# Loads of keys and values on GpSimd's queue, attention one step later, and four unsplit steps

## The chip, the cores and the metric

The kernel runs on one core of one Trainium2 chip. The metric is the device time of one execution in microseconds. The core's engines are TensorE (PE in the profile; its weight loads are PEld), VectorE (DVE), ScalarE (ACT), GpSimd (POOL) and SyncE (SP). SyncE does no arithmetic here; it issues DMAs. GpSimd and ScalarE can issue DMAs too, each through a queue of its own.

## The reference

Three stages follow one another, all in float32.

- Attention with pooled keys and values: q, k and v have the shape (8 batches, 8 heads, 576 positions, 64). Keys and values are averaged over groups of 8 positions, which leaves 72 of each. Then softmax(q k^T / 8) v per batch and head.
- A first layer on the 4608 tokens x 512 features: `h = x @ w_in` (512 x 2048), then g = h for h >= 1, 0 for h <= -1, and (h + 1)^2 / 4 in between, then `g @ w_out` (2048 x 512).
- A second layer of the same sizes with g = max(h, 0)^2.

## The kernel before

**Split products.** A float32 product on TensorE would be slow, so each operand is split into a high part that TensorE takes in its faster format and a low part, the rest. A product is then three matmuls: high x high, low x high, high x low. The high part is made by ScalarE (a copy) and the low part by VectorE (a subtraction). In the trace these are `wihi` and `wilo` for the first weight of a layer, `wohi` and `wolo` for the second (both L237 and L241), `xhi` and `xlo` for the tokens (L541, L542) and `gh` and `gl` for the activations (L749, L755). `WHOLE` (L26) says how many of the very first steps leave the second product unsplit: those multiply `gw` and `wo` in plain float32 (L775), and make none of `gh`, `gl`, `wohi`, `wolo`.

**Steps.** The first layer is done in steps: 9 blocks of 512 tokens x 16 slices of 128 hidden features, 144 steps, and then the first block of the second layer in 16 more. In step s TensorE does the first product of step s (`gemm1`, L714, 12 matmuls) and the second product of step s - 2 (`gemm2`, L786, 12 matmuls, or L775). The result of a block stands in four PSUM banks (`acc`) until its last step. The rest of the second layer (from about 1000 us) has another form and isn't touched.

**Weights of the first layer.** They come in pieces of 512 KB through SyncE's queue (`st`, `stx`, L135 and L140), and ScalarE and VectorE convert them to their final values (`convert_w`, L147) in the first 16 steps, some 8 pieces ahead of the step that uses them. The second layer's weights are converted later, from step 28 on; there an integer addition runs on GpSimd (L182), ScalarE copies its result (`cb`, L192) and it is stored for later.

**Attention beside the steps.** The 4608 tokens are 36 tiles of 128. Tiles 0 to 3 are done ahead of step 0, in an order written out by hand (`before`). The tiles from the fourth on are put into the steps: each step has two slots, 2s after its first product and 2s + 1 after its second. A tile t has units for the scores of heads 0 to 3 and 4 to 7 (`s`), for the next tile's queries (`q`), and for its output (`x`). For tiles 4 to 7 the slots are listed; from tile 8 on they follow from one number `c` (L562): scores at 2c and 2c + 2, queries at 2c + 4, output at 2c + 11. The output of a block's four tiles is the input of that block's first product, so the last of them has to be out before step 16j for block j. Where a tile is the first with a new batch, its keys' units stand at 2c - 2 and 2c - 1, and the pooling of that batch's keys and values (`pool_kv`, VectorE, L332 and L333) at slots counted from c (`pool_at`).

**Keys and values.** `load_kv` loads a pair of heads into one of three buffers `kv` (a fourth place is borrowed for the last pair of batch 0). For batches 0 and 1 the pooling is done by TensorE with a matrix of ones (`pk` L346 for keys, `pv` L367 for values), and each pair is two transfers, a large one (L303, 256 KB) and one of the last 64 positions (L313, 32 KB; batch 0 has one for all heads). For batches 2 to 7 a pair is one transfer (L317, 288 KB) and VectorE pools. A load waits until its buffer has been read for the last time.

**What sets the order.** The program order is that of the Python code, but a planner rearranges it: it keeps a priority by program order, assumes a duration for each instruction, and puts on each engine and each queue what it believes ready first. That order is then fixed, and on the chip every engine and every queue works strictly in it. So an instruction that waits holds all that stands behind it in its queue, and a unit may run some steps ahead of its slot.

Of the kernel before, what the change touches and what calls it, by code (L numbers as in the profile page):

```python
# [22 lines left out]
LEAD = 8  # L23
HEADS = 3

WHOLE = 6  # L26

TURNED = 8

# [5 lines left out]
def pooled_attention_moe_moe(  # L35
# [11 lines left out]
    nc = tc.nc  # L47
# [8 lines left out]
    KF = DFF // P  # L56
# [235 lines left out]
    def load_kv(nm, b, p):  # L292
        if b == 0 and p == NP - 1:

            a = cv.tile([P, 2, POOL * D], F32, tag="st", name="kv")
        else:
            a = kvp.tile([P if b < ON_PE else SP, 2, POOL * D], F32, tag="kv", name="kv")
        src = k if nm == "k" else v
        kv_t[nm, b, p] = a
        if b < ON_PE:  # L300

            src = src[b, 2 * p:2 * p + 2]
            nc.sync.dma_start(  # L303
                out=a[:, :, 0:BY * D], in_=src[:, 0:BY * P, :].rearrange("h (s r) d -> s h (r d)", r=BY)
            )
            if b == 0:
                if p == (1 if nm == "k" else 0):
                    rest[nm] = gp.tile([S - BY * P, H, D], F32, tag="gh", name="rest")
                    nc.sync.dma_start(
                        out=rest[nm], in_=(k if nm == "k" else v)[b, :, BY * P:S, :].rearrange("h s d -> s h d")  # L310
                    )
                return
            nc.sync.dma_start(  # L313
                out=a[0:S - BY * P, :, BY * D:(BY + 1) * D], in_=src[:, BY * P:S, :].rearrange("h s d -> s h d")
            )
            return
        nc.sync.dma_start(  # L317
            out=a, in_=src[b, 2 * p:2 * p + 2].rearrange("h (s r) d -> s h (r d)", r=POOL)
        )

# [228 lines left out]
    TB0 = TB // P  # L549
# [6 lines left out]
    for t in range(TB0, NTILE):  # L556

        if t < 2 * TB0:
            c = (2, 5, 8, 10)[t - TB0]
            at_s0, at_s1, at_q, at_x = 2 * c, 2 * c + 1, 2 * c + 2, (15, 19, 25, 29)[t - TB0]  # L560
        else:
            c = KF - 4 + 4 * (t - 2 * TB0)  # L562
            at_s0, at_s1, at_q, at_x = 2 * c, 2 * c + 2, 2 * c + 4, 2 * c + 11
        todo = {at_s0: ("s", t, 0), at_s1: ("s", t, 1), at_x: ("x", t)}
        if t == 2 * TB0 - 1:
            todo[at_x - 2] = ("all", ("p", t, 0), ("p", t, 1))
        if t + 1 < NTILE:
            todo[at_q] = ("q", t + 1)
        if t in first_tile:
            b = first_tile.index(t)  # L570
            todo.update({2 * c - 2 + i // 2: ("k", b, i) for i in (0, 2)})
            if b < ON_PE:
                todo.update({at_v: ("v", b, i) for at_v, i in zip((7, 9), (0, 2))})
            for i in range(2 * NP if b >= ON_PE else 0):
                at_p = 2 * (c + i - 8) + (i >= NP) * 8
                pool_at[at_p] = 2 * NP * b + i + 1
        assert not slots.keys() & todo.keys()
        slots.update(todo)

        assert 2 * KF * (t // TB0 - 2) <= at_x - 2 < at_x + 2 < 2 * KF * (t // TB0), t  # L580
# [9 lines left out]
    def load_kv_to(n):  # L590
        while kv_loaded[0] < min(n, len(kv_order)):
            load_kv(*kv_order[kv_loaded[0]])
            kv_loaded[0] += 1
# [78 lines left out]
    def whole(kind, s):  # L672

        return kind == "o" and s < WHOLE

# [411 lines left out]
    def temp(tag, bufs=2):  # L1087
        return tp.tile([P, TB], F32, tag=tag, name=tag, bufs=bufs)
# [109 lines left out]
    for n, u in enumerate(units):  # L1198
        kind, b, i, g = u
# [9 lines left out]
        if kind == "i":  # L1209
            if i == 5:  # L1210
                after_i(b, 5, g)

                c = temp("c", 3)
# [42 lines left out]
```

## Time and profile before

| | |
|---|---|
| time, median of 3 runs | 1620.85 us (1620.62 to 1620.98) |
| profiled execution | 1620.48 us, its span 1618.7 us |
| TensorE busy | 1612.0 us (100%), 7866 matmuls |
| weight loads of TensorE | 1317.1 us (81%) |
| VectorE busy | 1246.5 us (77%) |
| ScalarE busy | 905.0 us (56%) |
| GpSimd busy | 54.1 us (3%), 60 instructions |
| DMA moved | 283.91 MB, 175 GB/s on the mean |
| SyncE's queue (q1) | 249072 packets, 282.16 MB |
| granted TensorE clock | full in all slices of the span |

The span is the time from the first to the last instruction; the few microseconds around it belong to the execution too. Matmuls overlap in the records: one of 512 columns is recorded with about 390 ns, but follows the one before it after some 227 ns, so a busy share of TensorE near 100% means that it never stood, and the length of a group is read from the starts. An unsplit float32 matmul is recorded as two. GpSimd issues no DMA in this kernel: all loads and stores but four at the end go through SyncE's queue.

### The profile page before, as it was taken

The page shows a single profiled execution, that of the slowest core. Times are in us where ns is not written, and L with a number is a line of the kernel's source. Part 1 is how long each engine was busy: PE and PEld are TensorE (multiplying, and loading weights), DVE is VectorE, ACT ScalarE, POOL GpSimd, SP SyncE. Part 2 cuts the span into 40 slices and gives each one's busy share as a digit, 9 for nine tenths or more (in the row PEclk, how much of TensorE's full clock was granted, in tenths as well). Part 3 has the DMA queues.
Part 4 walks back from the last instruction along what each step waited for, and adds up shares of the span by engine and source line. Part 5 has one row for each costly group of instructions (what it writes and reads, how often), then busy time and mean ns, then how long its engine had stood idle before and what let it go on. Part 6 is the DMA issues. An engine that isn't in the chain of part 4 may idle for free.

```text
span 1618.7 us, 23331 instructions
## 1 busy us (share of the span) xinstructions
PE 1612.0 (100%) x7866; PEld 1317.1 (81%) x7866; DVE 1246.5 (77%) x2231; ACT 905.0 (56%) x1676; POOL 54.1 (3%) x60
## 2 busy tenths in 40 slices
PE   9999999999999999999999999999999999999998
PEld 7678888888878888888888888888888888888887
DVE  6999889898898999998975542578558855975585
ACT  7786566666666666666775532345335533553353
POOL 0000000100000000010100000000000000000000
PEclk9999999999999999999999999999999999999999
DMA  9753344554454554543560474566776776758565
GB/s 257 233 176 99 96 127 151 167 163 120 133 157 147 170 146 132 170 136 134 183 220 7 133 264 148 193 218 207 200 251 220 217 229 210 222 184 252 194 206 142
DMA packets 250279, 283.91 MB, mean 175 GB/s; under 512 B 123440, under 2 KB 155824, under 8 KB 250160
## 3 DMA queue, kind: packets, MB, share of 16 engines
q1 hardware_dynamic: 249072, 282.16, 56.5%
q8 instruction: 63, 1.03, 0.3%
q14 instruction: 56, 0.46, 0.1%
q10 hardware_dynamic: 1088, 0.26, 0.1%
HBM read 217.71 MB, written 64.62 MB: 174 GB/s over the span
## 4 chain that ended last, share of the span: by engine, by line
PE 98%; DMA 1%; DVE 1%; SPq 0%; issue 0%; ACT 0%; DVEq 0%; ACTq 0%
PE ph L714 27%; PE acc L786 26%; PE cp L1072 11%; PE dp L1081 10%; PE dq L1081 5%; PE cr L1072 5%; PE dr L1081 3%; PE cq L1072 3%; PE pss L411 2%; PE px L529 2%; PE acc L775 1%; PE pv L367 0%; DMA kv<-in_v_dram 0%; DMA w<-w2i 0%; PE pk L346 0%; PE dp L1182 0%
## 5 line engine op out<-in xcount | busy, mean ns | idle before, releaser
L714 PE MATMUL ph<-xhi,wihi 128*128 128x512 f32 x576 | 229.9, 399 | 0.0
L1029 ACT ACTIVATE gh<-g 128x512 fp32r<-128x512 f32 x224 | 139.9, 630 | 152.9 <-DVE g L1098 47.9
L714 PE MATMUL ph<-xlo,wihi 128*128 128x512 f32 x576 | 225.0, 391 | 0.0
L714 PE MATMUL ph<-xhi,wilo 128*128 128x512 f32 x576 | 224.9, 390 | 0.0
L786 PE MATMUL acc<-gh,wohi 128*128 128x512 f32 x552 | 222.6, 403 | 0.0
L786 PE MATMUL acc<-gl,wohi 128*128 128x512 f32 x552 | 216.1, 391 | 0.0
L786 PE MATMUL acc<-gh,wolo 128*128 128x512 f32 x552 | 215.5, 390 | 0.0
L821 DVE TENSOR_TENSOR gl<-g,gh 128x512 fp32r<-128x512 f32 x224 | 151.9, 689 | 49.7 <-ACT gh L1029 48.2
L1072 PE MATMUL cp<-x,w 128*128 128x512 f32 x768 | 186.4, 390 | 0.2 <-DMA w<-w2i 0.2
L1072 PEld LDWEIGHTS cp<-x,w 128*128 128x128 f32 x768 | 143.9, 188 | 31.5 <-ACT s L1094 1.4
L237 ACT ACTIVATE wihi<-wi 128x512 fp32r<-128x512 f32 x144 | 90.6, 629 | 123.4 <-PE ph L714 122.7
L1081 PE MATMUL dp<-gh,w 128*128 128x512 f32 x496 | 156.8, 390 | 0.0
L241 DVE TENSOR_TENSOR wilo<-wi,wihi 128x512 fp32r<-128x512 f32 x144 | 101.9, 708 | 46.5 <-ACT wihi L237 43.5
L714 PEld LDWEIGHTS ph<-xhi,wihi 128*128 128x128 f32 x576 | 108.1, 188 | 26.7 <-issue 3.8
L714 PEld LDWEIGHTS ph<-xhi,wilo 128*128 128x128 f32 x576 | 108.2, 188 | 23.1 <-issue 0.2
L714 PEld LDWEIGHTS ph<-xlo,wihi 128*128 128x128 f32 x576 | 108.3, 188 | 21.1 <-issue 0.2
L755 DVE TENSOR_TENSOR gl<-g,gh 128x512 fp32r<-128x512 f32 x154 | 107.0, 695 | 23.1 <-ACT gh L749 20.4
L749 ACT ACTIVATE gh<-g 128x512 fp32r<-128x512 f32 x138 | 86.8, 629 | 64.4 <-DVE g L747 63.5
L1094 ACT ACTIVATE s<-cp 128x512 f32<-128x512 f32 x96 | 57.1, 595 | 116.8 <-PE cp L1072 116.0
L786 PEld LDWEIGHTS acc<-gl,wohi 128*128 128x128 f32 x552 | 103.7, 188 | 22.9
L786 PEld LDWEIGHTS acc<-gh,wohi 128*128 128x128 f32 x552 | 103.8, 188 | 20.9 <-issue 0.6
L786 PEld LDWEIGHTS acc<-gh,wolo 128*128 128x128 f32 x552 | 103.9, 188 | 19.9
(161 smaller groups left out, 2953.3 us busy)
## 6 DMA issues: line engine op xcount, KB each, us to landing
w<-w2i SPq DMA_DIRECT2D x224, 256.0 KB
w<-w2o SPq DMA_DIRECT2D x224, 256.0 KB
w2i<-cb SPq DMA_DIRECT2D x32, 512.0 KB
w2o<-cb SPq DMA_DIRECT2D x32, 512.0 KB
st<-in_moe_w_in_dram SPq DMA_DIRECT2D x30, 512.0 KB
st<-in_moe_w_out_dram SPq DMA_DIRECT2D x30, 512.0 KB
pd<-pad SPq DMA_DIRECT2D x31, 384.0 KB
z<-pd SPq DMA_DIRECT2D x93, 128.0 KB
```

What stands on the lines that cost most here:

```text
L237: nc.scalar.activation(out=hi, in_=src, func=AF.Copy)
L241: eng.tensor_tensor(out=lo, in0=src, in1=hi.bitcast(F32), op=ALU.subtract)
L411: nc.tensor.matmul(out=pss[off:off + n, i, :], lhsT=qT[t][:, p, off:off + n], rhs=kbd[b % 2][:, p, :], start=True, stop=True,)
L714: nc.tensor.matmul(out=ph, lhsT=a[:, kk % a.shape[1], :], rhs=c[:, kk, :], start=(i == 0), stop=(i == 3 * KD - 1))
L749: act(out=gh, in_=g, func=AF.Copy)
L755: nc.vector.tensor_tensor(out=gl, in0=g, in1=gh.bitcast(F32), op=ALU.subtract)
L786: nc.tensor.matmul(out=o, lhsT=lhsT, rhs=rhs, start=(f == 0 and x == 0), stop=(f == KF - 1 and x == 2),)
L821: tt(out=out, in0=a, in1=b, op=ALU.subtract)
L1029: act(out=hi, in_=a, func=AF.Copy)
L1072: nc.tensor.matmul(out=out[0], lhsT=w[:, a, k, :], rhs=xq[b, i][c][:, k, :], start=(n == 0 and i in (1, 2, 7)), stop=(n == 5), skip_group_ ...
L1081: nc.tensor.matmul(out=out[d], lhsT=w[:, a, d, :], rhs=x[c], start=(g == 0 and n == 0 and i in (1, 2, 7, 4)), stop=(g == NG - 1 and n == 2 ...
L1094: act(out=snaps[key], in_=a, func=AF.Copy)
```

## The change

Three edits:

1. `WHOLE` goes from 6 to 4, so steps 4 and 5 do their second product split.
2. In `load_kv` the queue is SyncE's for batch 0 and GpSimd's for batches 1 to 7. All six calls of `load_kv`'s transfers use it; buffers, sizes and order stay.
3. `c` of the tiles from the eighth on is one larger, so all their units, the keys' units and the pooling of batches 2 to 7 stand one step (two slots) later. The step at which the attention's buffers are given back moves along, since it is worked out from the last slot.

```diff
-WHOLE = 6
+WHOLE = 4
...
         src = k if nm == "k" else v
+        queue = nc.sync if b == 0 else nc.gpsimd
         kv_t[nm, b, p] = a
         if b < ON_PE:
 
             src = src[b, 2 * p:2 * p + 2]
-            nc.sync.dma_start(
+            queue.dma_start(
                 out=a[:, :, 0:BY * D], in_=src[:, 0:BY * P, :].rearrange("h (s r) d -> s h (r d)", r=BY)
             )
             if b == 0:
                 if p == (1 if nm == "k" else 0):
                     rest[nm] = gp.tile([S - BY * P, H, D], F32, tag="gh", name="rest")
-                    nc.sync.dma_start(
+                    queue.dma_start(
                         out=rest[nm], in_=(k if nm == "k" else v)[b, :, BY * P:S, :].rearrange("h s d -> s h d")
                     )
                 return
-            nc.sync.dma_start(
+            queue.dma_start(
                 out=a[0:S - BY * P, :, BY * D:(BY + 1) * D], in_=src[:, BY * P:S, :].rearrange("h s d -> s h d")
             )
             return
-        nc.sync.dma_start(
+        queue.dma_start(
             out=a, in_=src[b, 2 * p:2 * p + 2].rearrange("h (s r) d -> s h (r d)", r=POOL)
         )
...
         else:
-            c = KF - 4 + 4 * (t - 2 * TB0)
+            c = KF - 3 + 4 * (t - 2 * TB0)
             at_s0, at_s1, at_q, at_x = 2 * c, 2 * c + 2, 2 * c + 4, 2 * c + 11
```

## Rows read from the trace of the kernel before

**Rows 1.** Busy us (instructions) of each engine in three stretches, clock, DMA.
```profile
0.00:40.00 40.00, 38.15 (x334) 31.60 (x335) 26.27 (x62) 28.39 (x80) 2.03 (x10) 1.00 0.95 260
40.00:160.00 120.00, 119.90 (x664) 88.99 (x664) 114.59 (x220) 91.63 (x217) 0.52 (x2) 1.00 0.58 168
160.00:820.00 660.00, 660.00 (x3352) 539.37 (x3351) 588.05 (x1136) 428.90 (x781) 50.41 (x46) 1.00 0.48 147
...
```
**Rows 2.** Chain of waits in order of time, 60 to 100 us: start, us, what.
```profile
63.65 6.36 DMA kv<-in_v_dram
...
82.09 3.44 PE acc L775 x8
88.27 3.43 PE acc L775 x8
...
96.23 2.77 PE acc L786 x12
```
**Rows 3.** Groups of instructions on ScalarE and VectorE: busy us, mean ns, idle before.
```profile
L749 ACT ACTIVATE gh<-g 128x512 fp32r<-128x512 f32 x138 | 86.8, 629 | 64.4 <-DVE g L747 63.5
L237 ACT ACTIVATE wohi<-wo 128x512 fp32r<-128x512 f32 x138 | 85.8, 622 | 13.0 <-PE acc L786 11.1 <-DVE wo L182 1.5
...
L755 DVE TENSOR_TENSOR gl<-g,gh 128x512 fp32r<-128x512 f32 x154 | 107.0, 695 | 23.1 <-ACT gh L749 20.4
L241 DVE TENSOR_TENSOR wolo<-wo,wohi 128x512 fp32r<-128x512 f32 x138 | 96.6, 700 | 5.9 <-ACT wohi L237 5.6
```
**Rows 4.** VectorE in order of time, 71 to 143 us: start us, us, instruction.
```profile
71.31 0.68 DVE L332 TENSOR_TENSOR kv<-kv 72x512 f32<-72x512 f32 x1
...
141.36 0.74 DVE L469 TENSOR_REDUCE sm<-pn 128x8 f32<-128x576 f32 x1
142.01 0.68 DVE L542 TENSOR_TENSOR xlo<-px,xhi 128x512 fp32r<-128x512 f32 x1
```
**Rows 5.** TensorE in order of time around step 16.
```profile
145.11 0.48 PE L714 MATMUL ph<-xhi,wihi 128*128 128x512 f32 x1
```
**Rows 6.** VectorE in order of time, 330 to 338 us.
```profile
330.79 0.67 DVE L542 TENSOR_TENSOR xlo<-px,xhi 128x512 fp32r<-128x512 f32 x1
...
337.24 0.69 DVE L755 TENSOR_TENSOR gl<-g,gh 128x512 fp32r<-128x512 f32 x1
```
**Rows 7.** TensorE in order of time, 339 to 343 us.
```profile
339.18 0.39 PE L714 MATMUL ph<-xhi,wihi 128*128 128x512 f32 x1
...
342.29 0.49 PE L786 MATMUL acc<-gh,wohi 128*128 128x512 f32 x1
```
**Rows 8.** SyncE's queue in order of time, 42 to 64 us.
```profile
42.32 0.38 SPq L303 DMA_DIRECT2D kv<-in_k_dram  x1
...
63.65 0.38 SPq L303 DMA_DIRECT2D kv<-in_v_dram  x1
```
**Rows 9.** Waits of SyncE's queue: us in total, times, longest us.
```profile
SPq L303 <- PE pk L346: 12.1, 2, 11.0
```
**Rows 10.** TensorE in order of time, pooling of batch 1.
```profile
46.61 0.90 PE L346 MATMUL pk<-pad,kv 128*64 128x64 f32 x20
...
59.53 2.79 PE L367 MATMUL pv<-kv,pad 128*72 128x128 f32 x20
...
68.56 2.96 PE L367 MATMUL pv<-kv,pad 128*72 128x128 f32 x20
```
**Rows 11.** Instructions on the tile kv: ns min/median/max, first and last start, forms.
```profile
L332 DVE TENSOR_TENSOR kv<-kv x96: 373/636/1808, 71.3 to 685.7; 72x512 f32<-72x512 f32 x48, 72x256 f32<-72x256 f32 x48
...
L317 SPq DMA_DIRECT2D kv<-in_k_dram x24: 307/400/752, 64.8 to 610.0; - x24
```
**Rows 12.** Instructions of line 182 on GpSimd: ns min/median/max, first and last start.
```profile
L182 POOL TENSOR_TENSOR z<-st,z x16: 1306/1542/2832, 214.8 to 798.2; 128x512 int32<-128x512 int32 x16
```
**Rows 13.** Waits between engines: us in total, times, longest us.
```profile
ACT cb L192 <- POOL z L182: 38.6, 30, 3.2
```

## The prediction

> **What bounds the kernel now.** I read the busy time by stretch first. TensorE is busy for 119.90 of the 120 us from 40 to 160 us, and for 660.00 of 660 us after that, at a granted clock of 1.00 [rows 1]; it loses 1.85 us before 40 us, while the first tiles are prepared. The chain of waits read in order of time says the same: it is a file of matmul groups, with one DMA in it between 60 and 100 us, a load of values that takes 6.36 us [rows 2]. So only two things can pay: fewer TensorE cycles, or the few waits that TensorE still has. And only one thing can cost: work that reaches TensorE too late. VectorE is the engine to watch: 114.59 us of 120 between 40 and 160 us, when the first layer's weights are converted, and 588.05 of 660 us after that [rows 1].
>
> All sums are made against the profiled execution's own 1620.48 us (its span of 1618.70 us and 1.78 us around it). The median of the runs is 1620.85 us, 0.37 us more, and the final number is put on that.
>
> **Part 1: four unsplit steps instead of six.** The second product of an unsplit step is a group of 8 records on TensorE of 3.43 or 3.44 us; the first split one is 12 records of 2.77 us [rows 2]. Steps 4 and 5 (the groups at 82.09 and 88.27 us) change from one to the other: 2 x (3.43 - 2.77) = 1.32 us less. Each of the two steps pays for it elsewhere: two more activations (0.629 us for `gh`, 0.622 us for `wohi`) and two more VectorE operations (0.695 us for `gl`, 0.700 us for `wolo`) [rows 3]. That is 2.50 us for ScalarE, which has 28.37 us idle from 40 to 160 us, and 2.79 us for VectorE, which has 5.41 us [rows 1]. What must be late for TensorE to notice? The tightest hand-over that I found there is the last tile of the second token block (t = 7): its `xlo` starts at 142.01 us and takes 0.68 us, and the first product of step 16, which reads it, starts at 145.11 us, so 2.42 us are left [rows 4, 5]. TensorE gets there 1.32 us earlier, which leaves 1.10 us. If nothing absorbed the 2.79 us of VectorE, TensorE would stand for 2.79 - 1.10 = 1.69 us at step 16. Two things absorb it: the idle 5.41 us, and work of tile 8 that part 2 moves behind this point, such as the sum of its softmax rows (0.74 us at 141.36 us) [rows 4]. The bounds of the stall are 0 and 1.69 us; I take 0, since what is idle is twice what is added. So part 1 is -1.32 us, and +0.37 us at worst.
>
> **Part 2: tiles from the eighth one step later.** No instruction is added or removed. Scores, turned queries, outputs and pooling of each tile get slots that lie one step further on. A step lasts 6.06 us in this stage (step 16's first product starts at 145.11 us, step 48's at 339.18 us: 194.07 / 32) [rows 5, 7]. The hand-over that gets tighter is again that of a block's last tile: tile 15's `xlo` ends at 330.79 + 0.67 = 331.46 us and is read from 339.18 us on, 7.72 us later [rows 6, 7]; one step less leaves 1.66 us. Tile 7, which this part does not move, already sits at just that distance (slot 29, two steps ahead of step 16), in the stretch in which VectorE is fullest, and still has its 2.42 us. So I price part 2 at nothing; the bounds are 0 and, if VectorE ran one 1.8 us operation late at each of the seven later blocks [rows 11], 7 x (1.8 - 1.66) = 1.0 us. Its help for part 1 is not certain either: the planner issues what is ready, and a pooling of batch 2 ran at 71.31 us, in step 5, though its slot is in step 8 [rows 4].
>
> **Part 3: 64 loads of keys and values move from SyncE's queue to GpSimd's.** These are 16 of batch 1 (8 large, 8 small) and 48 of batches 2 to 7. On SyncE the queue stood for 12.1 us in total, 11.0 us in one piece, in front of a load whose buffer TensorE still read [rows 9]; weight loads behind it will now pass. They had landed in time anyway, since TensorE did not wait, so this frees nothing that the path sees. What is on the path are the two loads that come just in time. The first is the last pair of values of batch 1: it was issued at 63.65 us, its buffer is free from about the middle of the pooling at 59.53 us (59.53 + 2.79 / 2 = 60.9 us), and the pooling at 68.56 us that waits for it took 2.96 us where the same one before took 2.79 us [rows 8, 10]. Issued some 2.7 us earlier, it no longer holds anyone: -0.17 us. The second is the last pair of keys of batch 1, issued at 42.32 us, when its buffer came free, and read at 46.61 us, so it lands within 4.29 us [rows 8, 10]. Nothing in the trace is a DMA issued by GpSimd, so its price needs bounds. Below: an issue as cheap as SyncE's (0.31 us at least, 0.40 us median) [rows 11], and nothing late. Above: a load that takes the 6.36 us of the slow one [rows 2], which makes TensorE stand for 6.36 - 4.29 = 2.07 us at 46.61 us. I take 0, by the nearer row: nothing else is queued for DMA at 42 us, and the 6.36 us belong to a load that stood behind two weight loads.
>
> On GpSimd itself the loads meet the integer additions of the second layer's conversion (1.54 us each in the larger form, up to 2.83 us) [rows 12]. ScalarE waits for these already, 38.6 us in 30 waits, 3.2 us at most [rows 13]. Behind ScalarE stand `gh`, then `gl`; a tight `gl` of that stage ends at 337.93 us and is read at 342.29 us, 4.36 us later [rows 6, 7]. An issue of 0.4 us or even 2.83 us ahead of an addition stays inside that. GpSimd is busy for 50.41 of 660 us [rows 1], so its own load is no limit. Part 3 is -0.17 us.
>
> [...]
>
> **The sum.** -1.32 + 0 - 0.17 = -1.49 us: 1618.99 us for the profiled execution, 1619.36 us on the median.
>
> **Rivals.**
> *The gain is eaten early.* A just-in-time load or hand-over becomes late before 160 us: the keys at 46.61 us by up to 2.07 us, or step 16 by up to 1.69 us. For it: VectorE has only 5.41 us of air there, and the load has no more than 4.29 us. Against it: the static order on TensorE is planned anew, and other products can stand ahead of the late one. Time: 1620.85 - 1.49 + 2.07 = 1621.4 us, with both 1623.1 us. [...]
>
> *Slower: GpSimd's queue holds the additions.* From 200 to 820 us, a load whose buffer is not yet free stands in GpSimd's queue ahead of an addition; ScalarE waits for it at its copy, and `gh` behind it comes too late. It decides from a hold of about 4.4 us. For it: SyncE's queue has been held for 11.0 us by such a load [rows 9]. Against it: the planner orders the queue by when it believes buffers are free. One hold of 5.4 us in each of the six batches costs 6 x 1.0 = 6 us (1625.4 us); holds of 11.0 us cost 6 x 6.6 = 40 us (1659 us).
>
> *Faster at the start.* With batch 1 off SyncE's queue the first weights and queries come sooner, and the 1.85 us that TensorE loses before 40 us go as well: 1617.5 us. Against it: ScalarE and VectorE prepare the first tiles there, and loads at the very start are those of batch 0, which stay.
>
> *The change doesn't do what it says.* The planner runs pooling as early as before; then VectorE gets no relief, and the time is that of the eaten gain or of the forecast.
>
> **How the numbers follow.** Forecast 58%, gain eaten 20% (the fourth rival is split between these two), slower 13%, faster at the start 9%. About 0.2% (3.2 us) is what a measurement of this kernel can tell from no change: below 1617.6 us is faster, above 1624.1 us slower. The forecast lies in between with some room for a changed order of the groups on TensorE, the eaten gain with nearly all its span; so faster 10% (nearly all of it the third rival), same 75%, slower 15% (the second rival, and 2% of both early stalls and more). The range 1617.3 to 1624.0 us leaves out about 7% below and 15% above.
>
> **What would show it.** Right: 32 records of line 775 instead of 48, and 12-record groups of 2.77 us for steps 4 and 5; no DMA wait at the pooling near 68 us; TensorE's busy share at 119.9 of 120 us from 40 to 160 us; step 16 begins about 1.4 us earlier, and the distance to the second layer's start stays as it was. Wrong: TensorE idle on line 346 with a DMA of keys as releaser; `xlo` as releaser at the first product of step 16 or 32; GpSimd's additions released by its own queue or by a DMA and ScalarE's waits for them well over 38.6 us; VectorE operations of two inputs longer than now. The prediction falls if the time from 160 to 820 us changes by more than 1 us, for I priced it at nothing.

## The result, and the profile after

The changed kernel takes **1639.64 us** (median of 5 runs, 1636.88 to 1642.47), against 1620.85 us (1620.45 to 1623.87) for the kernel before on the same chip: ratio 1.0111, 95% interval [1.0094, 1.0129]. It is slower by 18.8 us on the medians, where 1.5 us faster was forecast. The profiled execution took 1642.47 us (span 1640.7 us), 22 us more than the one of before.

The same three stretches as in [rows 1], now of the changed kernel (busy us and instructions of PE, PEld, DVE, ACT and POOL; then granted clock, DMA share, GB/s):

```profile
0.00:40.00 40.00, 36.99 (x332) 30.72 (x333) 26.38 (x62) 29.70 (x82) 6.16 (x16) 1.00 0.94 260
40.00:160.00 120.00, 115.27 (x643) 87.22 (x642) 109.86 (x211) 89.88 (x214) 13.63 (x20) 1.00 0.60 165
160.00:820.00 660.00, 647.47 (x3279) 526.60 (x3278) 580.05 (x1118) 408.89 (x760) 75.65 (x84) 0.99 0.48 142
```

TensorE, which never stood from 160 to 820 us, now stands there for 12.53 us, and for 4.73 us from 40 to 160 us instead of 0.10. Who it waits for leads back to the moved loads. The waits of the changed kernel (us in total, times, longest), of which the first answers to [rows 13]; the last three were not there before:

```profile
ACT cb L192 <- POOL z L182: 56.6, 30, 3.8
ACT gh L750 <- DVE g L748: 114.2, 94, 7.0
DVE kv L333 <- DMA kv<-in_k_dram: 26.1, 14, 4.2
DVE kv L333 <- DMA kv<-in_v_dram: 7.9, 5, 2.7
PE acc L787 <- DVE o L806: 5.2, 2, 4.1
```

The wait of `gh` in the kernel before:

```profile
ACT gh L749 <- DVE g L747: 63.5, 83, 2.2
```

(From `load_kv` on, each line number is one higher than before.) VectorE stands in front of its pooling for 34.0 us in 19 waits, because keys and values of batches 2 to 7 have not landed. The additions on the tile `kv` that answer to [rows 11] (ns min/median/max, first and last start), then the 48 loads of line 318 and their time from issue to landing:

```profile
L333 DVE TENSOR_TENSOR kv<-kv x96: 370/528/1639, 77.9 to 638.7; 72x512 f32<-72x512 f32 x48, 72x256 f32<-72x256 f32 x48
```
```profile
L318 POOL DMA_DIRECT2D kv<-in_k_dram x24: 693/693/721, 63.2 to 606.6; - x24
L318 POOL DMA_DIRECT2D kv<-in_v_dram x24: 693/693/1038, 113.3 to 628.0; - x24
...
DMA to landing us min/median/max: 3.5/5.1/10.5
```

An issue costs GpSimd 0.69 us where it cost SyncE's queue 0.40, and the load lands 3.5 to 10.5 us after the start of its issue. The profile has no landing times for the same loads on SyncE's queue. What the rows of both kernels do show is the distance that the order leaves from the start of an issue to the first addition: under 7 us for 4 of the 48 loads before, without a wait, and for 15 of them now. The additions themselves have not become longer (528 ns in the middle, 636 before).

**One stall from cause to cost.** GpSimd, VectorE and TensorE of the changed kernel in order of time (start us, us, instruction; in brackets the idle time before it and what ended it), one block for each engine:

```profile
250.99 0.70 POOL L318 DMA_DIRECT2D kv<-in_k_dram  x1 [3.88 <-DVE kp L334]
251.68 0.69 POOL L318 DMA_DIRECT2D kv<-in_v_dram  x1
```
```profile
253.49 0.68 DVE L241 TENSOR_TENSOR wolo<-wo,wohi 128x512 fp32r<-128x512 f32 x1
258.37 1.14 DVE L333 TENSOR_TENSOR kv<-kv 72x512 f32<-72x512 f32 x2 [4.19 <-DMA kv<-in_k_dram]
261.39 0.69 DVE L333 TENSOR_TENSOR kv<-kv 72x512 f32<-72x512 f32 x1 [1.88 <-DMA kv<-in_v_dram]
...
265.30 0.64 DVE L756 TENSOR_TENSOR gl<-g,gh 128x512 fp32r<-128x512 f32 x1
265.87 1.27 DVE L806 COPY o<-acc 128x512 f32<-128x512 f32 x2
```
```profile
262.13 0.40 PE L787 MATMUL acc<-gl,wohi 128*128 128x512 f32 x1
266.59 0.79 PE L787 MATMUL acc<-gh,wohi 128*128 128x512 f32 x1 [4.07 <-DVE o L806]
267.18 0.63 PE L787 MATMUL acc<-gh,wolo 128*128 128x512 f32 x1
267.61 0.63 PE L787 MATMUL acc<-gl,wohi 128*128 128x512 f32 x1
...
270.17 0.63 PE L787 MATMUL acc<-gl,wohi 128*128 128x512 f32 x1
270.73 1.46 PE L530 MATMUL px<-aT,vp 72*64 72x128 f32 x16
```

The keys are issued at 250.99 us. VectorE, whose order is fixed, reaches their pooling at 254.2 us and stands for 4.19 us, then 1.88 us more for the values. All that is queued behind comes 6 us late: `g`, `gl`, and at a block boundary the copy of the finished block out of `acc`, for which TensorE waits 4.07 us. Then the granted clock is down to 0.50. The same place in stretches (columns as above):

```profile
250.00:258.00 8.00, 8.00 (x42) 6.18 (x41) 3.67 (x8) 5.81 (x13) 2.08 (x3) 1.00 1.01 253
258.00:262.00 4.00, 4.00 (x24) 2.98 (x23) 1.72 (x3) 0.00 (x0) 0.00 (x0) 1.00 0.63 149
262.00:267.00 5.00, 0.93 (x4) 0.49 (x3) 5.00 (x10) 3.12 (x7) 0.69 (x1) 0.77 0.19 59
267.00:271.00 4.00, 4.00 (x12) 2.68 (x13) 4.00 (x9) 2.71 (x6) 0.00 (x0) 0.50 0.53 197
```

From 267 to 271 us the granted clock is 0.50. Nine matmuls take 270.73 - 266.59 = 4.14 us where nine at 0.227 us take 2.04, so the stall of 4.07 us costs some 6.2 us, and none of it shows as idle time beyond the 4.07. The first row bears on why the keys took more than 7 us: the DMA engines are busy throughout from 250 to 258 us (share 1.01), when GpSimd issued three loads within 2.4 us. How much of a late landing is this crowding and how much the queue was not tested.

**Where the 22 us are.** For each step of the first layer, the start of its first matmul in the changed kernel less the same in the kernel before, worked out from the trace's rows of L714 and L715:

```
step        0    16    32    48    64    80    96   112   128   144
us later  0.4   4.0   4.0  11.5  13.5  18.4  19.8  19.8  21.2  22.0
```

Some 4 us are lost before step 16, 15.8 us from step 16 to step 112, in jumps, and 2.2 us after that. Of the 15.8 us, 11.4 are idle time of TensorE and some 2 the slower matmuls above. The clock fell only behind this one stall: the other nine from 160 to 820 us lasted 0.39 to 1.84 us, and the granted clock stayed at 1.00 behind them.

### The profile page after: what moved, and what is told of

Read it like the earlier page. It is cut to its first block, busy times and chain, and to the rows that moved or that the text cites. A ratio compares the mean times of both kernels' runs of the same rounds, so it can differ in the third digit from the quotient of the medians.

```text
span 1640.7 us, 23406 instructions
## 1 busy us (share of the span) xinstructions
PE 1615.2 (98%) x7874; PEld 1319.0 (80%) x7874; DVE 1251.1 (76%) x2235; ACT 899.0 (55%) x1680; POOL 98.6 (6%) x124
## 4 chain that ended last, share of the span: by engine, by line
PE 61%; DVE 4%; ACT 1%; DMA 1%; issue 1%; POOL 0%; SPq 0%; POOLq 0%; DVEq 0%; ACTq 0%
PE acc L787 12%; PE ph L715 11%; PE cp L1073 11%; PE dp L1082 10%; PE dq L1082 5%; PE cr L1073 5%; PE cq L1073 3%; PE dr L1082 3%; PE px L530 1%; PE pss L412 1%; DVE g L748 0%; DMA kv<-in_k_dram 0%; POOL z L182 0%; DVE wolo L241 0%; DVE wilo L241 0%
## 5 line engine op out<-in xcount | busy, mean ns | idle before, releaser
L787 PE MATMUL acc<-gh,wohi 128*128 128x512 f32 x560 | 226.7, 405 | 5.2 <-DVE o L806 5.2
L715 PE MATMUL ph<-xhi,wihi 128*128 128x512 f32 x576 | 230.2, 400 | 1.2 <-ACT xhi L542 0.7
L715 PE MATMUL ph<-xlo,wihi 128*128 128x512 f32 x576 | 225.3, 391 | 1.4 <-DVE xlo L543 1.4
L715 PE MATMUL ph<-xhi,wilo 128*128 128x512 f32 x576 | 224.8, 390 | 0.0
L787 PE MATMUL acc<-gl,wohi 128*128 128x512 f32 x560 | 219.9, 393 | 0.0
L787 PE MATMUL acc<-gh,wolo 128*128 128x512 f32 x560 | 219.4, 392 | 0.0
L715 PEld LDWEIGHTS ph<-xhi,wihi 128*128 128x128 f32 x576 | 108.1, 188 | 29.3 <-issue 3.4
L715 PEld LDWEIGHTS ph<-xlo,wihi 128*128 128x128 f32 x576 | 108.3, 188 | 22.8 <-DVE xlo L543 2.1
L715 PEld LDWEIGHTS ph<-xhi,wilo 128*128 128x128 f32 x576 | 108.2, 188 | 22.9
```

The lines of the kernel that those rows point to most:

```text
L715: nc.tensor.matmul(out=ph, lhsT=a[:, kk % a.shape[1], :], rhs=c[:, kk, :], start=(i == 0), stop=(i == 3 * KD - 1))
L787: nc.tensor.matmul(out=o, lhsT=lhsT, rhs=rhs, start=(f == 0 and x == 0), stop=(f == KF - 1 and x == 2),)
```

## The experiments

Theory after the result: the planner, which knows the loads as early on their own queue, orders VectorE's pooling close behind them; they land later than it believes, VectorE stands, and TensorE with it. Rivals: one of the other two edits, or the three together; GpSimd's additions held by the loads in their own queue; the mere presence of 48 loads issued by GpSimd. Every ratio below is against the kernel before, run in the same session on the same chip; its median there was 1622.3 to 1623.4 us, for a reason told in the last section.

### Which edit

**no_q**: the change with all loads on SyncE's queue.

```diff
-        queue = nc.sync if b == 0 else nc.gpsimd
+        queue = nc.sync
```

> All loads back on SyncE's queue; four unsplit steps and the later tiles stay. Theory A (the loads on GpSimd's queue land late, VectorE stands for them in its fixed order, TensorE then stands for VectorE): 1619.4 us, between 1618 and 1621, and no wait of VectorE for a DMA of kv. Theory B (VectorE has too much to do with four unsplit steps): at least 1630 us still. Theory C (the later slots put pooling and the copies out of PSUM into one step): at least 1630 us still.

Measured: 1625.09 us, ratio 1.0008 [0.9998, 1.0018]. All but a tenth of a per cent of the loss goes with the queue, so theories B and C fall; the time is above theory A's 1621 us. In its profile the two edits left don't add up to a gain. The lag against the kernel before goes from 0.6 us at step 0 to -0.4 at step 8, is 1.0 us at step 16, ahead of which TensorE stands for 1.01 us (it waits for `aT`) and for 0.48 us, and 3.5 us at step 143. So some of what the changed kernel loses after step 16 is not the queue's.

**q_only**: the kernel before with the queue alone (`WHOLE` = 6, `c = KF - 4 ...`).

```diff
-WHOLE = 4
+WHOLE = 6
...
-            c = KF - 3 + 4 * (t - 2 * TB0)
+            c = KF - 4 + 4 * (t - 2 * TB0)
```

> Only the queue changes: six unsplit steps, tiles where they were. Theory A: 1632 to 1645 us with 20 us or more of VectorE's waits for DMAs of kv. Theory B or C: within 2 us of before. Theory D (the queue hurts only together with the later slots): within 3 us of before, and VectorE's waits for DMAs of kv under 10 us.

Measured: 1632.71 us, ratio 1.0064 [1.0046, 1.0081]; VectorE waits 18.3 us for keys and 8.3 us for values. The queue alone costs more than half of the loss; the rest comes when the other edits are added.

**whole_only** and **shift_only**: each of the other edits alone, all loads on SyncE's queue (the edits against the kernel before).

```diff
-WHOLE = 6
+WHOLE = 4
```

> Only four unsplit steps, on SyncE's queue and with the tiles where they were. My sum of the prediction: 1620.9 - 1.3 = 1619.5 us, at worst 1621.2 us (a stall of 1.7 us at step 16). Theory B: 1630 us or more.

```diff
-            c = KF - 4 + 4 * (t - 2 * TB0)
+            c = KF - 3 + 4 * (t - 2 * TB0)
```

> Only the tiles from the eighth on one step later, on SyncE's queue, six unsplit steps. My sum: 1620.9 us, at worst 1621.9 us. Theory C: 1630 us or more, with TensorE waiting for VectorE's copies out of PSUM at the starts of blocks.

Measured: 1622.13 us, ratio 1.0000 [0.9991, 1.0010], and 1623.28 us, ratio 1.0006 [0.9992, 1.0019]. Neither can be told from no change. In the profile of whole_only steps 0 to 8 are 1.6 us shorter than before (the lag against it goes from 3.8 to 2.2 us), where part 1 put 1.32 us; the median doesn't resolve them.

**q_shift**: queue and later slots, without the edit of `WHOLE`.

```diff
-WHOLE = 4
+WHOLE = 6
```

> Kernel after, with the six unsplit steps of before: queue and later slots, without part 1. It asks which part turns the queue's own +0.64% into +1.11%. Theory L (the later slots: the pooling of a block's second batch runs a step later and meets the block's last tile and VectorE's copies of the second product): 1.010 to 1.012, and VectorE waits over 25 us for keys and values. Theory W (fewer unsplit steps take VectorE's room before 160 us, and what is late there stays late): 1.005 to 1.007, the waits near the 26.6 us of the queue alone.

Measured: 1636.51 us, ratio 1.0094 [1.0076, 1.0112]; VectorE waits 16.0 us for keys and 8.3 us for values. The ratio lies between the two forecasts, nearer to theory L, whose mark of over 25 us in waits is just missed. So the later slots, harmless by themselves, make the queue dearer (1.0064 to 1.0094); the intervals touch, and the split of the rest is not settled.

### Which loads

**b27_pool** and **b1_pool**: the changed kernel with only batches 2 to 7, or only batch 1, on GpSimd's queue.

```diff
-        queue = nc.sync if b == 0 else nc.gpsimd
+        queue = nc.gpsimd if b > 1 else nc.sync
```

> As the changed kernel, but batch 1's 16 loads are on SyncE's queue; GpSimd's has the 48 of batches 2 to 7. Theory A (VectorE stands for late loads of batches 2 to 7): most of the loss stays, 1633 to 1642 us, with 25 us or more of VectorE's waits for DMAs of kv. Rival E (the loss comes from the crowded start, where batch 1's loads take DMA time from the weights): 1626 us or less.

```diff
-        queue = nc.sync if b == 0 else nc.gpsimd
+        queue = nc.gpsimd if b == 1 else nc.sync
```

> As the changed kernel, but only batch 1's 16 loads are on GpSimd's queue. Theory A: 1620 to 1626 us, with a loss of at most 4 us, all of it before step 16. Rival E: 1633 us or more.

Measured: 1637.27 us, ratio 1.0088 [1.0069, 1.0106], and 1624.06 us, ratio 1.0012 [1.0001, 1.0023]. From 160 to 820 us:

```profile
160.00:820.00 660.00, 651.51 (x3302) 530.11 (x3302) 580.93 (x1127) 410.98 (x763) 77.87 (x86) 1.00 0.49 144
```
```profile
160.00:820.00 660.00, 660.00 (x3354) 538.74 (x3353) 595.85 (x1140) 425.39 (x778) 51.37 (x44) 1.00 0.48 145
```

The first row is b27_pool, the second b1_pool: the stalls of the long middle belong to batches 2 to 7 alone. Batch 1, the one that the prediction worked out load by load, can't be told from nothing: b1_pool has 1.0012, and no_q, without the queue, 1.0008.

### Taking the cause away

**q_held**: the changed kernel, with one more rule for the planner: the pooling of a pair may not be put ahead of the last gate operation (`g`) issued so far. The loads stay on their queue; the rule is on VectorE's order alone (the buffers come free later by it, so the last load is issued at 696 us instead of 628).

```diff
+        with tc.issue_after(last_g[-1].ins):
+            for w in (4 * D, 2 * D):
+                nc.vector.tensor_tensor(out=a[:, :, 0:w], in0=a[:, :, 0:w], in1=a[:, :, w:2 * w], op=ALU.add)
+            nc.vector.tensor_tensor(out=o, in0=a[:, :, 0:D], in1=a[:, :, D:2 * D], op=ALU.add)
...
-                nc.vector.scalar_tensor_tensor(out=g, in0=ph, scalar=1.0, in1=u, op0=ALU.max, op1=ALU.min)
+                last_g.append(nc.vector.scalar_tensor_tensor(out=g, in0=ph, scalar=1.0, in1=u, op0=ALU.max, op1=ALU.min))
```

> The changed kernel, queue and all, but VectorE's pooling of each pair is held behind the activation of the step ahead of its slot, so the planner can't put it right behind its load. Theory A1 (GpSimd's loads are not too slow as such, but the planner, with the queue of their own, puts pooling too close behind them): 1619 to 1625 us, VectorE's waits for DMAs of kv under 6 us. Rival F (DMAs that GpSimd issues slow down other transfers or VectorE's operations, whatever the order): 1632 us or more still.

Measured: 1630.05 us, ratio 1.0042 [1.0027, 1.0058], between the two forecasts: slower than theory A1 had it, quicker than rival F. VectorE's pooling in the changed kernel and in q_held (busy us, mean ns, then the idle time before it and its releasers), and q_held's stretch from 160 to 820 us:

```profile
L333 DVE TENSOR_TENSOR kv<-kv 72x512 f32<-72x512 f32 (+1 forms) x96 | 52.7, 556 | 34.2 <-DMA kv<-in_k_dram 26.1 <-DMA kv<-in_v_dram 7.9
```
```profile
L335 DVE TENSOR_TENSOR kv<-kv 72x512 f32<-72x512 f32 x96 | 54.2, 564 | 0.2
```
```profile
160.00:820.00 660.00, 659.46 (x3349) 537.60 (x3348) 595.64 (x1146) 426.21 (x778) 79.55 (x89) 1.00 0.49 146
```

34.2 us of standing become 0.2, and TensorE's 12.53 us of idle time become 0.54, with all 64 loads still on GpSimd's queue, and each issue as slow as before. The shortest distance from a load's issue to its first addition is now 13.7 us, and the slowest of the 48 landings takes 9.7 us. So neither the additions in GpSimd's queue nor the presence of its loads makes the stalls of the middle: the order does. Its profile is 8.8 us late in all: 3.6 us before step 0, in a stretch that varies by itself (last section), 2.7 us from step 0 to step 16, and 2.5 us after that, as many as no_q loses there without the queue.

**sync_held**: the same hold with all loads on SyncE's queue, a control.

```diff
-        queue = nc.sync if b == 0 else nc.gpsimd
+        queue = nc.sync
```

> Kernel after with all loads back on SyncE's queue, and with the held pooling: the hold without the queue. Theory H (the early loss of the held kernels comes from the hold, which has the first 160 us ordered anew): 1626 to 1632 us, ratio 1.002 to 1.006, and step 16 begins 5 us or more later than before. Theory Q (it comes from GpSimd's queue): as without the hold (ratio 1.0008), 1622 to 1626 us.

Measured: 1622.75 us, ratio 1.0003 [0.9994, 1.0012]. The hold by itself costs nothing, so theory H falls in this form: what the held kernels still lose comes only with GpSimd's queue. Whether the hold makes the queue dearer before step 16 this run can't tell.

**b27_held**: the hold, with batch 1 back on SyncE's queue.

```diff
-        queue = nc.sync if b == 0 else nc.gpsimd
+        queue = nc.gpsimd if b > 1 else nc.sync
```

> Kernel after, with two edits: the loads of batch 1 go back to SyncE's queue (those of batches 2 to 7 stay on GpSimd's), and the pooling of a pair may not be put ahead of the last gate operation issued so far, so that it is not planned right behind its load. Theory P (VectorE's planned order stands for loads that are not there yet): both shares of the loss are taken away, 9.9 us (the run with pooling held, 1630.0, against 1639.6) and about 2.4 us (the run with batch 1 alone on GpSimd), so 1621 to 1625 us, ratio 0.999 to 1.003; VectorE waits less than 3 us for keys and values, TensorE is busy for over 659 of the 660 us from 160 to 820 us. [...]

Measured: 1629.55 us, ratio 1.0047 [1.0034, 1.0061]. The 1621 to 1625 us of theory P are missed, though both of its marks in the middle are there (659.30 of 660 us, no wait of VectorE for keys or values). The time is that of its rival, theory G: that the 48 loads on GpSimd's queue cost something by themselves, at least 0.4%, so 1627 us or more. The profile shows another place, the last values of batch 1. TensorE's wait for them, the load in the chain of waits (start us, us), and the stretches around it:

```profile
75.98 2.61 PE L370 MATMUL pv<-kv,pad 128*72 128x128 f32 x10 [2.35 <-DMA kv<-in_v_dram]
```
```profile
67.32 8.61 DMA kv<-in_v_dram
```
```profile
72.00:76.00 4.00, 1.65 (x12) 1.02 (x10) 3.82 (x7) 2.04 (x4) 0.70 (x1) 0.97 1.13 182
76.00:80.00 4.00, 4.00 (x14) 3.08 (x15) 2.05 (x4) 0.38 (x1) 0.88 (x2) 0.50 1.11 291
```

This load was just in time before: 6.36 us [rows 2]. On SyncE's queue the keys of batch 2 followed it; on a queue of their own they are issued ahead of it (66.31 us on GpSimd, 67.32 us on SyncE), the DMA engines are busy throughout (share 1.13), and it takes 8.61 us. That lead is not the cause by itself: b27_pool and b37_held have it too, 1.01 us in both, and there TensorE stands for 0.59 and 0.48 us, as it does for 0.53 us in no_q, where the keys follow. Why the load takes so long here is open. A stall of 2.35 us is again followed by a granted clock of 0.50 (76 to 80 us): steps 4 to 6 lose 5.2 us.

**b37_held** and **q3_held**: the hold only from batch 3 on, in b27_held and in q_held.

```diff
-        with tc.issue_after(last_g[-1].ins):
+        with tc.issue_after(last_g[-1 if b > 2 else 0].ins):
```

> Kernel b27_held with the hold only from batch 3 on: batches 2 to 7 on GpSimd's queue, batch 1 on SyncE's, later slots, four unsplit steps. Theory H: the early loss goes (step 16 within 2 us of the run with batch 1 on SyncE and no hold, 1.5 us) and the mid-stage stays held (2 to 5 us lost from step 16 to 144, against 13.2 without the hold), so 1623 to 1628 us, ratio 1.001 to 1.004. Theory Q: still 1.004 or more.

> Kernel after with the hold only from batch 3 on, batch 1 on GpSimd's queue too. By theory H: early loss as in the changed kernel (4.0 us at step 16), 2 to 5 us in the middle instead of 18, so 1625 to 1630 us, ratio 1.002 to 1.005. If the stalls in the middle are not due to the packed pooling, it stays near 1.011.

Measured: 1629.08 us (six runs from 1624.86 to 1633.02), ratio 1.0047 [1.0033, 1.0061], and 1625.75 us, ratio 1.0026 [1.0016, 1.0036]. The second is as theory H forecast: with all 64 loads on GpSimd's queue and one rule more, 1.11% becomes 0.26%, which also leaves outside the interval the 0.4% that theory G put on the loads by themselves. The first is as theory Q forecast; its profiled run, the quickest of the six, shows 1.0 us lost up to step 16 and 2.4 us after that, and the same load of values with 6.75 us and a stall of 0.5 us. That the slower runs have the 8 us load of b27_held is possible, but no profile of them shows it.

### Other queues and a dead end

**act_q**: the changed kernel with the 64 loads on ScalarE's queue instead of GpSimd's.

```diff
-        queue = nc.sync if b == 0 else nc.gpsimd
+        queue = nc.sync if b == 0 else nc.scalar
```

> [...] Theory P (any queue on which the planner sees the loads as issued at once lets it pack the pooling close behind them): VectorE waits more than 10 us for keys and values again, ratio 1.004 to 1.015. Theory S (the slow landing of GpSimd's loads, 5.1 us median, is what is missing in the plan): loads land within 4 us, VectorE waits less than 5 us, ratio 0.998 to 1.003. If ScalarE's own work is held by a load whose buffer is not free, gh waits and the ratio is over 1.015.

Measured: 1631.12 us, ratio 1.0051 [1.0037, 1.0066]. The plan is packed just as closely: from a load's issue to its first addition it leaves under 7 us for 20 of the 48 loads (15 in the changed kernel, 4 before; worked out from the rows of the two lines). VectorE waits for keys and values again, as theory P had it, but less:

```profile
L333 DVE TENSOR_TENSOR kv<-kv 72x512 f32<-72x512 f32 (+1 forms) x96 | 52.4, 559 | 12.5 <-DMA kv<-in_k_dram 11.1 <-DMA kv<-in_v_dram 1.0
```
```profile
40.00:160.00 120.00, 115.02 (x600) 85.74 (x600) 111.69 (x212) 91.32 (x217) 0.52 (x2) 1.00 0.57 162
160.00:820.00 660.00, 658.84 (x3346) 536.79 (x3345) 591.80 (x1146) 421.00 (x778) 50.69 (x47) 1.00 0.49 146
```

TensorE loses 1.16 us in the middle, and most of the rest before 160 us. So a packed order alone gives the waits on another queue too, but fewer and shorter. The profile has no landing times for ScalarE's loads; those that VectorE waited for were used 4.2 to 7.0 us after their issue (11 loads), those of the changed kernel after 4.1 to 10.6 us (19). That GpSimd's loads land later, and that this makes the difference, is likely but not shown.

**dummy**: the kernel before, with 48 more DMAs on GpSimd's queue that copy the same keys and values of batches 2 to 7 to memory that nobody reads.

```diff
+        nc.gpsimd.dma_start(
+            out=dump[nm, b, p], in_=src[b, 2 * p:2 * p + 2].rearrange("h (s r) d -> s h (r d)", r=POOL)
+        )
```

> The kernel before with 48 loads more: GpSimd copies each pair of batches 2 to 7 to a place in DRAM that nobody reads, while SyncE loads the pairs as before. Theory A1: nobody waits for these, so within 4 us of before. Rival F: 1630 us or more, with longer transfers of SyncE's queue or longer VectorE operations.

Measured: 1647.66 us, ratio 1.0157 [1.0141, 1.0173]. It doesn't test what it was made for: as nothing holds the copies back to their batch, all were issued by 109 us, the first 8 by 8 us, and TensorE waits in this stretch.

```profile
16.20 1.12 PE L399 MATMUL pq<-ident,q 128*128 128x128 f32 x4 [5.64 <-DMA q<-in_q_dram]
70.19 0.79 PE L718 MATMUL ph<-xhi,wihi 128*128 128x512 f32 x1 [15.71 <-DVE gw L751]
```

From 160 to 820 us it stands for nothing. It shows only what this crowded start cost (from 40 to 160 us a DMA share of 0.82 where it was 0.58, and TensorE idle for 16.51 us instead of 0.10); the size that rival F had forecast came about, but not in the stretch that it was to explain.

**whole_0**: the kernel before with no unsplit step, a candidate.

```diff
-WHOLE = 6
+WHOLE = 0
```

> Kernel before with no unsplit step at all: all loads on SyncE, old slots. A candidate. By the price of part 1, 0.66 us for each of six steps: 1620.9 - 4.0 = 1616.9 us, ratio 0.9975, if ScalarE and VectorE have the room; step 8 then begins about 4 us earlier. Rival: VectorE is too full between 40 and 100 us (it had 5.41 us idle there and 120 from 40 to 160, six steps need 8.4 us): TensorE waits for gl, wolo or a tile, and the ratio is 1.000 to 1.006.

Measured: 1629.78 us, ratio 1.0038 [1.0025, 1.0052]: the rival. Up to step 10 the gain is there (the lag against before goes from 4.9 to 1.4 us, 3.5 of the 4.0 us priced); then TensorE waits for the high parts of the second weights, and step 16 is 10.4 us late:

```profile
127.83 1.20 PE L786 MATMUL acc<-gh,wohi 128*128 128x512 f32 x4 [2.76 <-ACT wohi L237]
...
146.97 1.19 PE L786 MATMUL acc<-gh,wohi 128*128 128x512 f32 x4 [1.22 <-ACT wohi L237]
```

None of the versions beats the kernel before.

## Why the prediction was wrong

- **Where it failed: part 3, "What is on the path are the two loads that come just in time."** The sum priced these two loads of batch 1 and put the 48 of batches 2 to 7 at nothing, without a reason of their own. It looked at when the loads landed in the old order, and not at what the planner does with a new queue: it moved the readers up behind the loads (under 7 us from issue to use for 15 loads instead of 4). Measured: 34.0 us of waits on VectorE and 12.53 us on TensorE from 160 to 820 us; from step 16 to step 112 the kernel lost 15.8 us. That the planner did so because it takes these loads for landed early is the reading that fits q_held; the planner's own times are not on record. Of the ratio, 1.0111 to 1.0026 goes with the hold from batch 3 on, and 1.0026 to 1.0008 with the rest of the queue.
- **Part 3, price of a load.** The term was 0, from SyncE's median of 0.40 us, with 6.36 us as the upper end. An issue took 0.69 us on GpSimd, 1.04 at most, and the 48 loads of 288 KB took from 3.5 to 10.5 us to land, 5.1 us at the median. The upper end was too low, and it was applied to one load of batch 1 instead of to all. What made landings long no run shows.
- **Part 1 was right where it was looked at.** 32 records on the unsplit line instead of 48, 1.6 us gained in whole_only up to step 8. whole_0 shows its limit: what it gives early is taken back before step 16, where TensorE waits for ScalarE. The stall that part 1 bounded by 1.69 us and took as 0 is there once part 2 is added: 1.01 and 0.48 us in no_q.
- **Part 2 was right alone and wrong in company.** 1.0006 [0.9992, 1.0019] by itself; with the queue the later slots go with a higher price (1.0064 to 1.0094, the intervals touch).
- **The slower rival named the queue, not the mechanism.** It held that loads would stand ahead of GpSimd's additions. ScalarE's waits for these went from 38.6 to 56.6 us, but to 3.8 us at the longest, under the 4.4 us from which the rival decides, and q_held, with the same queue, loses 0.54 us of TensorE in the middle.
- **The eaten gain came true in a form that it didn't name.** Neither the keys at 46 us nor the last values of batch 1 made TensorE wait. What came late were weights: the first of the two below were issued on SyncE's queue at 63.23 us, behind three loads on GpSimd's from 61.70 us on. ScalarE stood for both (start us, us, instruction):

```profile
72.66 0.66 ACT L160 ACTIVATE wo<-st 128x512 f32<-128x512 f32 x1 [5.98 <-DMA st<-in_moe_w_out_dram]
...
80.12 0.70 ACT L160 ACTIVATE wi<-st 128x512 f32<-128x512 f32 x1 [2.80 <-DMA st<-in_moe_w_in_dram]
```

  VectorE stands for 5.29 us behind it, and TensorE for 2.81 us from 81.95 us on. That this comes from sharing the DMA engines is argued from the times; b1_pool, at 1.0012, leaves room for about 0.1%.
- The prediction named what would overturn it: a change of more than 1 us from 160 to 820 us. That is what happened.

**What stays open**: how the rest that the queue costs with the pooling held (ratios of 1.0026 to 1.0047 in the four kernels) divides between late weights, the last values of batch 1 and the start of the kernel, and why b37_held, with fewer loads on GpSimd's queue, is slower than q3_held; what makes a load land late; and how much of the step from 1.0064 to 1.0111 is the later slots and how much `WHOLE`.

## What to carry to other kernels

Where a planner orders the engines, moving a transfer to another queue is also a change of the readers' order: ask what it will now put close behind the load, and price that by the landing time on the new queue (3.5 to 10.5 us here), for every load and not only for the tight ones. A queue in which loads stand behind others can be a useful brake (4 of the 48 loads were used within 7 us of their issue on the old queue, 15 on the new one); if it is taken away, hold the reader back by a rule of its own, which here gave most of the loss back but no gain. A stall of TensorE can cost more than its length: the longest one from 160 to 820 us, of 4.07 us, cost some 6.2 us, with a granted clock of 0.50 behind it; behind the nine others there, of 0.39 to 1.84 us, the clock stayed at 1.00.

## What the runs showed of the hardware

- A stall of 4.07 us in the changed kernel, and one of 2.35 us in b27_held, were each followed by about 4 us at a granted clock of 0.50. The first cost 6.2 us in all. A stall of 2.81 us in the changed kernel was followed by a clock of 1.00, so the length of a stall alone didn't decide it; what did is open:

```profile
84.76 0.66 PE L396 MATMUL pq<-ident,q 128*128 128x128 f32 x4 [2.81 <-ACT pn L445]
```
```profile
84.00:88.00 4.00, 3.24 (x16) 2.76 (x17) 4.00 (x9) 4.00 (x19) 0.00 (x0) 1.00 0.42 137
```

- The start of this program varies by itself. TensorE waits for the first queries at 8 to 10 us. The kernel before and whole_only have the same work there; in the first the wait is 0.62 us and the granted clock stays at 1.00, in the second it is 1.59 us and the clock falls to 0.58:

```profile
10.00:14.00 4.00, 4.00 (x56) 3.48 (x55) 1.38 (x4) 2.36 (x11) 0.00 (x0) 1.00 1.16 268
```
```profile
10.00:14.00 4.00, 3.75 (x30) 2.94 (x30) 0.63 (x2) 0.91 (x3) 0.00 (x0) 0.58 0.96 224
```

  Step 0 begins at 35.3 us in the first and 39.1 us in the second. In the profiles of eight of the 14 experiments other than dummy the clock fell there, to between 0.50 and 0.75 on the mean from 10 to 14 us, with and without loads on GpSimd's queue, and step 0 began 3.2 to 5.0 us late. That is the size by which the runs of the kernel before spread (1620.2 to 1626.1 us in the later sessions), and why effects of 1 to 2 us could not be told in these medians. The first of the moved loads, where there are any, is issued at 18.0 us or later, after the clock has fallen, so they are not the cause. What decides it is open: waits of 1.8 us were also seen with the clock staying at 1.00 (1.78 us in the changed kernel, 1.8 us in no_q).
